# Retention plus GELU feed-forward on one core: a new order of loads with a hold, block 0 in runs of 128 tokens, and the last block's products M6, M1, M7 by halves

## The chip, the cores and the metric

One Trainium2 chip, one of its cores. The metric is device time in microseconds (us) of one execution. The kernel before takes 296.12 us, the median of 3 runs (295.0 to 297.18).

## The reference

Inputs are q, k, v, each 8 batches x 8 heads x 576 positions x 64, and two weight matrices, `w_in` 512 x 2048 and `w_out` 2048 x 512, all float32.

```python
scores = scale * np.matmul(q, k.transpose(0, 1, 3, 2))
gamma = 1.0 - 2.0 ** (-5.0 - np.arange(H))
Dmat = np.where(rel >= 0, gamma[:, None, None] ** rel[None], 0.0)
attn = np.matmul(scores * Dmat[None], v)
x = attn.transpose(0, 2, 1, 3).reshape(B * S, H * D)
h = x @ w_in
out = (0.5 * h * (1.0 + erf(h / sqrt(2)))) @ w_out
```

So: a causal attention without softmax, whose mask decays with distance (retention), then a feed-forward layer with exact GELU over 4608 tokens of 512 values. The output is 4608 x 512, float32.

## The kernel before

**Units, groups, blocks.** A unit is 128 tokens. There are 36: batches go in pairs, and a pair has four chunks of 128 positions for each of its two batches, and one unit for the last 64 positions of both (units 10, 17, 26 and 35). Units 0 to 3 stand alone in groups 0 to 3; from unit 4 on the two units of one chunk form a group, so group 4 is units 4 and 5, group 5 is 6 and 7, group 6 is 8 and 9, group 7 is unit 10, group 8 is 11 and 12, group 9 is 13 and 14. A block is four units, 512 tokens, and there are nine.

**Attention of one group.** `load` brings q, k and v by DMA, issued on POOL and cast to bfloat16 on the way. q and k must be transposed: for groups 0 to 6 by TensorE (`turn`, with a copy out by VectorE or ScalarE), from group 7 on by two DMA transposes per group issued on SP (`turn_dma`). `scores` multiplies them on TensorE, `masked` applies the mask on VectorE (`ret`), `inner` multiplies with the values, `state` gathers the running state of keys and values, `cross` adds the contribution of the earlier chunks, `evacuate` writes the unit's transposed attention output into `xT`.

**Feed-forward.** `mlp1` multiplies `w_in` with `xT` (four matmuls for each 128 columns of `w_in`) and applies GELU on ScalarE. Block 0 takes it in runs of tokens 0 to 256, 256 to 384 and 384 to 512, block 1 in halves, later blocks whole. Block 0 then uses `mlp2`: plain matmuls with `w_out` that add up in one bank of PSUM for each unit (`ts`), in steps of two or four slices `m` of `w_out`; w_out number n holds slices 2n and 2n+1. Blocks 1 to 8 use seven products of half size (a Strassen scheme: M1 to M7, `part` with its four quarters, `after` for what follows each product), in the order M3, M4, M5, M2, M1, M6, M7. The sums of weights are made on VectorE by `sum_w`, those of GELU outputs by `sum_g`. M7 adds onto the bank of M1 (`behind`). In the last block M1 and M7 have a bank for each half; M7 goes half by half, M1 ends both halves together. `store` issues the output DMAs on SP.

**What sets the order.** The kernel is a planner in Python: it keeps a clock for each engine (`T`), costs for operations, a model of two DMA queues (`MOVE`, `SW_LATE`, `HW_LATE`, `SW_SHARE`), and writes out each engine's instructions in the order in which it thinks they can run. On the chip each engine runs its instructions in that fixed order and waits at semaphores where its plan was wrong. The loads up to unit 12, the weights, the constants (`io`) and the decay factors (`dq`) go in an order written out by hand, `ORDER` (lines 306 and 307), which `next_order` (309) takes from; later loads are appended by `reload` (525) as buffers come free. `fire` (786) issues loads, scaled values and DMA transposes; `mlp_pick` (764) chooses the next step of the feed-forward among the heads of the first four `runs`. A step of `mlp2` counts as ready (`mlp_ready`, 754) by this line, 761, in which `b_` and `c_` are the first and the end slice of the step:

```python
at = max(land_out.get((c_ - 1) // 2, 1e9) + SEM, max(g_at.get((t, m, ts), 1e9) for m in range(b_, c_)))
```

POOL issues at most eight loads ahead of the oldest that has not landed; SP issues transposes and stores in one queue. The steps by which the prediction goes: loads at lines 270 (`w_in`), 284 (`w_out`) and 297 (q, k, v); `turn` 387; transposes 398; `scores` 415, 424 and 434; `inner` 482 and 491; `state` 509; `cross` 541; `mlp1` 579; `mlp2` 614; `part` 712; the last sums 679; stores 604.

Of the kernel before, what the change touches and what calls it, by code (L numbers as in the profile page):

```python
# [10 lines left out]
BF16 = mybir.dt.bfloat16  # L11
# [6 lines left out]
def kernel(  # L18
# [14 lines left out]
    nc = tc.nc  # L33
# [35 lines left out]
    N_PE_TR = 7  # L69
# [109 lines left out]

    SW_LATE, HW_LATE, SW_SHARE = 4.6, 2.5, 0.48  # L180
    MOVE = {"wi": 1.28, "wo": 1.37, "ld": 0.845, "short": 0.42, "turn": 1.82, "store": 0.85}
    queues = ([], [])
# [81 lines left out]
    def load(what, i):  # L264
# [26 lines left out]
        for jj in (j,) if j is not None else range(2):  # L291
# [8 lines left out]
            else:  # L300
# [4 lines left out]
    cast_due = {("q", 0): (loaded[0][0][:, 0], first["q32"]), ("k", 0): (loaded[0][0][:, 1], first["k32"])}  # L305
    ORDER = ("k1 q1 wi0 io v0 k2 v2 q2 v1 k3 wi1 q3 wi2 wi3 wi4 k4 v3 q5 k5 wo0 wi5 wi7 wi6 q4 q6 wo1 v4 v5 wo2 "
             "wo3 k7 q7 q8 k6 wo4 dq2 q9 wo5 v6 k9 k11 v9 wo6 dq3 wo7 k8 v7 k10 v10 v12 q11 k12 q12 v8 v11 q10 dq4").split()

    def next_order():
        item = ORDER.pop(0)  # L310
        what = item.rstrip("0123456789")
        load(what, int(item[len(what):] or 0))

    def finish_later():
        while later:
            _, engine, dur, fn = later.pop(0)
            fn()
            on(engine, dur)

    while T["pool"] < 4.0:  # L320
        next_order()
# [71 lines left out]
    def turn_dma(n):  # L393
        qk, qkT = loaded[groups[n][0]][0], qkT_of(n)
        short = units[groups[n][0]][2] is None
        rows = TAIL if short else C
        for jj in range(2):
            nc.sync.dma_start(qkT[:, jj, :, 0:rows], qk[0:rows, jj].rearrange("p h j d -> p (h j d)"), transpose=True)
            ends = sg[n].setdefault("ends", {})

            def put(end, jj=jj):
                ends[jj] = end
                sg[n]["T"] = max(ends.values()) + SEM

            hw_dma(1.3, MOVE["turn"] * (0.5 if short else 1.0), max(land["qk"[jj], i] for i in groups[n]), put)

# [256 lines left out]
    def after(t, p, done, ts0, ts1, b, m):  # L663
# [13 lines left out]
        else:  # L677
            c = c11 if p == M7 else c22
            nc.vector.tensor_tensor(c, c, m, op=MINUS if p == M6 else ALU.add)  # L679
            at = on("dve", 0.26 * (ts1 - ts0) + 0.16, done)  # L680
        read_at[t, p] = at + SEM
        if p not in behind.values():
            release(b, at + SEM)
        if p == M6:
            for x in range(2):
                store(t, 2 + x, hi[:, x, :])
# [10 lines left out]
    def part(t, p, k):  # L697
        apart = t == N_BLK - 1 and p in (M1, M7)
        keys = [(t, bank_of[p], x) for x in range(1 + apart)]
        if p == M3 and k == 0:  # L700
            for x in range(2):
                o_tiles[t, x] = o_pool.tile([128, 2, d_model], FP32, tag=f"o{x}", name=f"o{x}")
        if k == 0 and p in begins:
            for key in keys:
                held_bank[key] = bank([128, 2 - apart, 256], FP32, "m")
        todo = [(mm, ts) for mm in range(2 * k, 2 * k + 2) for ts in range(2)]
        if apart and p == M7:
            todo = [(mm, k // 2) for mm in range(k % 2 * 4, k % 2 * 4 + 4)]
        for mm, ts in todo:
            a, w = factors(t, p, mm, ts)  # L710
            m = held_bank[keys[ts * apart]][1]
            nc.tensor.matmul(m[:, 0 if apart else ts, :], lhsT=a, rhs=w,  # L712
                             start=p in begins and mm == 0 and (apart or ts == 0),
                             stop=p not in behind.values() and mm == N_DF // 2 - 1, skip_group_check=True)
        done = pe(4 * 0.1092)
        if apart and (p == M1 and k == 3 or p == M7 and k % 2):
            for ts in range(2) if p == M1 else (k // 2,):
                after(t, p, done, ts, ts + 1, *held_bank[keys[ts]])
        elif k == 3:
            after(t, p, done, 0, 2, *held_bank[keys[0]])  # L720

    def part_ready(t, p, k):
        mms = range(2 * k, 2 * k + 2)
        at = max(ws_at.get(mm, 1e9) for mm in mms)
        if p in (M3, M4):
            at = max([at] + [g_at.get((t, 2 * mm + x, ts), 1e9) for mm in mms for x in range(2) for ts in range(4)])
        else:
            n = {M2: 0, M5: 0, M1: 1}.get(p, 2)
            if p == M7 and t == N_BLK - 1:
                mms = range(N_DF // 2)  # L730
            at = max([at] + [gs_at.get((t, mm, n), 1e9) for mm in mms])
        if k == 0:
            at = max(at, read_at.get((t, behind[p]), 1e9) if p in behind
                     else free_time(1 + (p == M1 and t == N_BLK - 1)))
        return at
# [5 lines left out]
    for t in range(N_BLK):  # L741
        if t < 2:
            cuts = (0, 256, 384, 512) if t == 0 else (0, 256, 512)
            for lo, hi in zip(cuts, cuts[1:]):
# [6 lines left out]
        else:  # L751
            runs.append([("3", t, p, k) for p in range(7) for k in range(4)])

# [26 lines left out]
    nA = nB = nX = nT = nV = 0  # L780
    nD = N_PE_TR
    half = 0
# [3 lines left out]
    def fire():  # L786
        nonlocal nD, nV
        now = T["pe"]
        while ORDER and T["pool"] <= now + 1.5:
            next_order()  # L790
        while T["dve"] <= now + 1.5:
# [40 lines left out]
    while True:  # L832
# [6 lines left out]

        pick = mlp_pick(1 if runs and runs[0] and runs[0][0][1] > 1 else 4)  # L840
        head = pick[1][0] if pick else None
# [128 lines left out]
```

## Time and profile before

| what | value |
|---|---|
| median of 3 runs | 296.12 us (295.0 to 297.18) |
| the profiled execution | 295.88 us, its span 294.1 us |
| TensorE clock granted in it | 0.998 |
| matmuls busy | 282.1 us of the span |
| VectorE, ScalarE, POOL busy | 193.2, 131.5, 113.8 us |
| q0, DMAs issued on POOL | 18.10 MB |
| q1, DMAs issued on SP | 16.52 MB |

In the profile PE is the row of matmuls, PEld that of weight loads (they overlap), DVE is VectorE, ACT is ScalarE, POOL is GpSimd, SP the engine that issues transposes and stores (SPq: its queue). An arrow `out<-in` names tiles. "Time to landing" is from the start of an issue to the DMA's last part. All times are from the start of the span. Times of 0.25 us or less between matmuls of one step include places where a record is missing.

### The profile page before, as it was taken

How to read it: one execution, taken by the hardware profiler on the slowest of the kernel's cores; microseconds unless marked ns; L12 is line 12 of the kernel's file. 1: busy time of each engine (PE TensorE's matmuls, PEld its weight loads, DVE VectorE, ACT ScalarE, POOL GpSimd, SP SyncE). 2: the span in 40 equal slices, each digit the busy share in tenths (PEclk: the TensorE clock that was granted, in tenths of full speed). 3: DMA queues.
4: the chain of work that ended last, by engine and by line, in shares of the span. 5: the costliest groups of instructions: out<-in, count | busy, mean ns of one | idle time of the engine just before them, and what ended most of it. 6: DMA issues, size and time to landing. Idle time of an engine off the chain costs nothing.

```text
span 294.1 us, 7654 instructions
## 1 busy us (share of the span) xinstructions
PE 282.1 (96%) x3191; PEld 195.2 (66%) x3212; DVE 193.2 (66%) x455; ACT 131.5 (45%) x235; POOL 113.8 (39%) x143
## 2 busy tenths in 40 slices
PE   7999999997899999999999999999999999999993
PEld 2588766586785488558845785578557854874682
DVE  3762387987698983974497789754977385435532
ACT  5476444363215641574065414741554156416620
POOL 8977898975583246510784444000000000000000
PEclk9999999999999999999999999999999999999999
DMA  9999999999999999999999999990300040021013
GB/s 135 162 178 188 181 171 172 200 177 132 137 134 222 141 126 147 190 156 153 79 228 122 121 141 163 196 71 22 125 2 0 4 144 0 0 74 72 0 38 107
DMA packets 152066, 35.36 MB, mean 120 GB/s; under 512 B 141024, under 2 KB 147680, under 8 KB 152032
## 3 DMA queue, kind: packets, MB, share of 16 engines
q0 software_dynamic: 116832, 18.10, 96.0%
q1 hardware_dynamic: 34160, 16.52, 32.7%
q8 instruction: 25, 0.41, 0.6%
q10 hardware_dynamic: 1040, 0.26, 0.4%
q14 instruction: 9, 0.07, 0.1%
HBM read 36.70 MB, written 9.44 MB: 157 GB/s over the span
## 4 chain that ended last, share of the span: by engine, by line
PE 83%; DMA 10%; POOL 4%; issue 1%; DVE 0%; SPq 0%; POOLq 0%; DVEq 0%
PE hT L579 38%; PE m L712 31%; PE oT L614 4%; DMA qkT<-qk_ld 4%; DMA qk_ld<-in_q_dram 3%; DMA w_in<-in_moe_w_in_dram 3%; PE sc L434 3%; PE o_ps L491 3%; POOL qk L297 2%; POOL w_in L270 1%; PE o_ps L541 1%; PE u_ps L509 1%; POOL v_ld L297 1%; PE qk_ps L387 1%; PE sc L424 0%
## 5 line engine op out<-in xcount | busy, mean ns | idle before, releaser
L579 PE MATMUL hT<-xT,w_in 128*128 128x512 bf16 (+2 forms) x754 | 128.0, 325 | 1.0 <-issue 0.2
L586 ACT ACTIVATE g<-hT 128x512 bf16<-128x512 f32 (+1 forms) x152 | 86.8, 574 | 68.5 <-PE hT L579 63.0
L579 PEld LDWEIGHTS <-w_in 128*128 128x128 bf16 x768 | 68.8, 98 | 54.5 <-DMA w_in<-in_moe_w_in_dram 0.3
L712 PEld LDWEIGHTS <-gs 128*128 128x128 bf16 x640 | 62.5, 98 | 7.4
L297 POOL DMA_DIRECT2D v_ld<-in_v_dram x40 | 34.0, 856 | 25.9 <-DVE vh L467 7.0
L712 PE MATMUL m<-w_sum,gs 128*128 128x256 bf16 x384 | 43.4, 273 | 0.0
L457 DVE TENSOR_TENSOR ret<-sc,msk 128x512 bf16<-128x512 f32 x48 | 30.4, 683 | 14.1 <-PE sc L434 14.1
L297 POOL DMA_DIRECT2D qk_ld<-in_q_dram x36 | 30.4, 849 | 23.2 <-DMA qkT<-qk_ld 16.9
L297 POOL DMA_DIRECT2D qk_ld<-in_k_dram x36 | 30.5, 852 | 16.8 <-DMA qk_ld<-in_q_dram 14.8
L639 DVE TENSOR_TENSOR gs<-g 128x512 bf16<-128x512 bf16 x64 | 26.1, 421 | 13.5 <-ACT g L586 13.5
L712 PE MATMUL m<-w_out,gs 128*128 128x256 bf16 x256 | 29.6, 273 | 0.0
L712 PE MATMUL m<-w_sum,g 128*128 128x256 bf16 x256 | 29.6, 273 | 0.0
L712 PEld LDWEIGHTS <-g 128*128 128x128 bf16 x256 | 24.9, 98 | 4.5
L679 DVE TENSOR_TENSOR o<-o,m 128x512 f32<-128x512 f32 (+1 forms) x26 | 16.7, 646 | 16.7 <-PE m L712 16.4
L643 DVE TENSOR_TENSOR gs<-g 128x512 bf16<-128x512 bf16 x64 | 25.5, 418 | 0.0
L467 DVE TENSOR_TENSOR vh<-v_ld,dv 128x512 bf16<-128x512 bf16 x36 | 23.6, 683 | 1.3 <-DMA v_ld<-in_v_dram 1.3
L675 DVE TENSOR_TENSOR o<-o,m 128x512 f32<-128x512 f32 x16 | 11.0, 686 | 14.7 <-ACT o L674 14.7
L370 ACT CAST u_sb<-u_ps 128x512 bf16<-128x512 f32 x14 | 8.2, 585 | 25.3 <-PE u_ps L509 25.3
L560 DVE TENSOR_TENSOR xT<-o_ps,dqT 128x512 bf16<-128x512 f32 (+1 forms) x32 | 18.4, 616 | 1.4 <-PE o_ps L541 1.3
L674 ACT COPY o<-m 128x512 f32<-128x512 f32 x16 | 9.4, 585 | 21.1 <-PE m L712 21.1
L668 ACT COPY o<-m 128x512 f32<-128x512 f32 x16 | 9.4, 585 | 20.9 <-PE m L712 19.5
L641 DVE TENSOR_TENSOR gs<-g 128x256 bf16<-128x256 bf16 x64 | 17.2, 284 | 0.0
(72 smaller groups left out, 193.9 us busy)
## 6 DMA issues: line engine op xcount, KB each, us to landing
out_dram<-o SPq DMA_DIRECT2D x30, 256.0 KB, 4.9
v_ld<-in_v_dram POOLq DMA_DIRECT2D x32, 128.0 KB, 9.5
qk_ld<-in_k_dram POOLq DMA_DIRECT2D x28, 128.0 KB, 10.6
qk_ld<-in_q_dram POOLq DMA_DIRECT2D x28, 128.0 KB, 8.7
w_in<-in_moe_w_in_dram POOLq DMA_DIRECT2D x8, 256.0 KB, 7.6
w_out<-in_moe_w_out_dram POOLq DMA_DIRECT2D x8, 256.0 KB, 7.9
out_dram<-o SPq DMA_DIRECT2D x12, 128.0 KB, 2.4
qk_ld<-in_k_dram POOLq DMA_DIRECT2D x8, 64.0 KB, 11.9
```

What stands on the lines that cost most here:

```text
L297: nc.gpsimd.dma_start(dst, src[2 * bp + jj, :, ci * C:ci * C + n, :].rearrange("h s d -> s h d"))
L457: nc.vector.tensor_tensor(r, t, by, op=ALU.mult)
L467: nc.vector.tensor_tensor(vh, loaded[i][1], dv[:, :, ci:ci + 1].to_broadcast([128, H, D]), op=ALU.mult)
L560: nc.vector.tensor_tensor(x_of(i)[:, :, n * x:n * x + n], o, dqT[:, :, ci * C:ci * C + n], op=ALU.mult)
L579: nc.tensor.matmul(hT[:, m, :], lhsT=w[:, cc, o:o + 128], rhs=x_tiles[t][:, cc, lo:hi], start=(cc == 0), stop=(cc == N_DM - 1))
L586: nc.scalar.activation(g_tiles[t, m0 // 2][:, m0 % 2:m0 % 2 + n, lo:hi], hT, AF.Gelu)
L614: nc.tensor.matmul(oT, lhsT=g_tiles[t, m // 2][:, m % 2, cols], rhs=w_out_sb[m // 2][:, m % 2, :], start=(m == 0), stop=(m == N_DF - 1))
L639: nc.vector.tensor_tensor(s[:, 0:2].rearrange("p a b -> p (a b)"), g[:, 0, :], g[:, 1, :], op=ALU.add)
L641: nc.vector.tensor_tensor(s[:, 2], g[:, 0, LEFT], g[:, 1, RIGHT], op=ALU.add)
L643: nc.vector.tensor_tensor(s[:, 3:5], g[:, :, LEFT], g[:, :, RIGHT], op=MINUS)
L679: nc.vector.tensor_tensor(c, c, m, op=MINUS if p == M6 else ALU.add)
L712: nc.tensor.matmul(m[:, 0 if apart else ts, :], lhsT=a, rhs=w, start=p in begins and mm == 0 and (apart or ts == 0), stop=p not in behind. ...
```

## The change

- `ORDER` is another order of the same loads, with one new item, `h7`, ahead of the last load, v11. At `h7`, `next_order` stops until the transposes of group 7 (unit 10) have been given out, then puts a small copy from their result (tile `rest`) on POOL, which holds all later loads there until these transposes have landed.
- Block 0's `mlp1` goes in four runs of 128 tokens, and `mlp_pick` looks at five runs.
- In the last block the products go in the order M3, M4, M5, M2, M6, M1, M7; M1, too, goes half by half, and the stores of the lower output half follow M1's halves and not M6.
- The planner's numbers for the DMA queues change.

In the order that comes out for TensorE, `mlp2` for unit 2 of block 0 goes slices 8 to 12 and then (after the scores of group 5) 12 to 16 ahead of slices 8 to 16 of units 0 and 1; before, it followed them. The scores of group 7 stand ahead of the last three pieces of block 1's `mlp1` and of its first two quarters of M3; before, behind them. Loads around them, in the new order: ... w_out 3, k9, v6, w_out 5, w_out 7, k10, w_out 4, v9, w_out 6, k8, v7, ...

```diff
@@ -177,8 +177,8 @@
         nc.vector.tensor_tensor(s[:, 3:5], w[:, :, 0:256], w[:, :, 256:512], op=ALU.add)
         ws_at[i] = on("dve", 1.0, land_out[i]) + SEM
-    SW_LATE, HW_LATE, SW_SHARE = 4.6, 2.5, 0.48
-    MOVE = {"wi": 1.28, "wo": 1.37, "ld": 0.845, "short": 0.42, "turn": 1.82, "store": 0.85}
+    SW_LATE, HW_LATE, SW_SHARE = 4.65, 2.8, 0.455
+    MOVE = {"wi": 1.28, "wo": 1.37, "ld": 0.845, "short": 0.42, "turn": 1.88, "store": 0.9}
     queues = ([], [])
     moved = [0.0, [0, 0], [None, None]]
@@ -303,13 +303,23 @@
     tiles_of(0)
     land["q", 0], land["k", 0] = 4.5, 4.6
     cast_due = {("q", 0): (loaded[0][0][:, 0], first["q32"]), ("k", 0): (loaded[0][0][:, 1], first["k32"])}
-    ORDER = ("k1 q1 wi0 io v0 k2 v2 q2 v1 k3 wi1 q3 wi2 wi3 wi4 k4 v3 q5 k5 wo0 wi5 wi7 wi6 q4 q6 wo1 v4 v5 wo2 "
-             "wo3 k7 q7 q8 k6 wo4 dq2 q9 wo5 v6 k9 k11 v9 wo6 dq3 wo7 k8 v7 k10 v10 v12 q11 k12 q12 v8 v11 q10 dq4").split()
+    ORDER = ("q1 k2 io v0 wi0 v3 q3 k1 q2 wi1 k4 k3 v1 wi2 wi3 q5 v2 k5 wi4 wo0 q8 wi5 wo1 q4 wi7 wi6 v4 q6 q7 dq2 "
+             "k7 k11 wo2 v5 k6 q9 wo3 k9 v6 wo5 wo7 k10 wo4 v9 dq3 wo6 k8 v7 v10 q12 k12 dq4 v12 v8 q11 q10 h7 v11").split()
+
+    rest = const.tile([128, 2], BF16, name="rest")
     def next_order():
-        item = ORDER.pop(0)
-        what = item.rstrip("0123456789")
-        load(what, int(item[len(what):] or 0))
+        what = ORDER[0].rstrip("0123456789")
+        n = int(ORDER[0][len(what):] or 0)
+        if what == "h":
+            if n >= nD:
+                return False
+            nc.gpsimd.tensor_copy(rest, qkT_of(n)[:, :, 0, 0])
+            T["pool"] = max(T["pool"], sg[n]["T"]) + 0.2
+        else:
+            load(what, n)
+        ORDER.pop(0)
+        return True
     def finish_later():
         while later:
@@ -317,6 +327,7 @@
             fn()
             on(engine, dur)
+    nD = N_PE_TR
     while T["pool"] < 4.0:
         next_order()
     next_load = [group_of[12] + 1]
@@ -402,7 +413,7 @@
                 ends[jj] = end
                 sg[n]["T"] = max(ends.values()) + SEM
-            hw_dma(1.3, MOVE["turn"] * (0.5 if short else 1.0), max(land["qk"[jj], i] for i in groups[n]), put)
+            hw_dma(1.3, MOVE["turn"] * (0.62 if short else 1.0), max(land["qk"[jj], i] for i in groups[n]), put)
     def scores(n):
         g = groups[n]
@@ -678,11 +689,11 @@
             c = c11 if p == M7 else c22
             nc.vector.tensor_tensor(c, c, m, op=MINUS if p == M6 else ALU.add)
             at = on("dve", 0.26 * (ts1 - ts0) + 0.16, done)
-        read_at[t, p] = at + SEM
+        read_at[t, p, ts0] = at + SEM
         if p not in behind.values():
             release(b, at + SEM)
-        if p == M6:
-            for x in range(2):
+        if p == M1 if t == N_BLK - 1 else p == M6:
+            for x in range(ts0, ts1):
                 store(t, 2 + x, hi[:, x, :])
         if p == M5 and t == N_BLK - 1:
             for x in range(2):
@@ -704,7 +715,7 @@
             for key in keys:
                 held_bank[key] = bank([128, 2 - apart, 256], FP32, "m")
         todo = [(mm, ts) for mm in range(2 * k, 2 * k + 2) for ts in range(2)]
-        if apart and p == M7:
+        if apart:
             todo = [(mm, k // 2) for mm in range(k % 2 * 4, k % 2 * 4 + 4)]
         for mm, ts in todo:
             a, w = factors(t, p, mm, ts)
@@ -713,9 +724,8 @@
                              start=p in begins and mm == 0 and (apart or ts == 0),
                              stop=p not in behind.values() and mm == N_DF // 2 - 1, skip_group_check=True)
         done = pe(4 * 0.1092)
-        if apart and (p == M1 and k == 3 or p == M7 and k % 2):
-            for ts in range(2) if p == M1 else (k // 2,):
-                after(t, p, done, ts, ts + 1, *held_bank[keys[ts]])
+        if apart and k % 2:
+            after(t, p, done, k // 2, k // 2 + 1, *held_bank[keys[k // 2]])
         elif k == 3:
             after(t, p, done, 0, 2, *held_bank[keys[0]])
@@ -726,12 +736,13 @@
             at = max([at] + [g_at.get((t, 2 * mm + x, ts), 1e9) for mm in mms for x in range(2) for ts in range(4)])
         else:
             n = {M2: 0, M5: 0, M1: 1}.get(p, 2)
-            if p == M7 and t == N_BLK - 1:
+            if p in (M1, M7) and t == N_BLK - 1:
                 mms = range(N_DF // 2)
             at = max([at] + [gs_at.get((t, mm, n), 1e9) for mm in mms])
-        if k == 0:
-            at = max(at, read_at.get((t, behind[p]), 1e9) if p in behind
-                     else free_time(1 + (p == M1 and t == N_BLK - 1)))
+        if p in behind and (k == 0 or k == 2 and p == M7 and t == N_BLK - 1):
+            at = max(at, read_at.get((t, behind[p], k // 2), 1e9))
+        elif k == 0:
+            at = max(at, free_time(1 + (p == M1 and t == N_BLK - 1)))
         return at
     def x_ready(t, lo, hi):
@@ -740,7 +751,7 @@
     runs = []
     for t in range(N_BLK):
         if t < 2:
-            cuts = (0, 256, 384, 512) if t == 0 else (0, 256, 512)
+            cuts = (0, 128, 256, 384, 512) if t == 0 else (0, 256, 512)
             for lo, hi in zip(cuts, cuts[1:]):
                 runs.append([("1", t, m, 2, lo, hi) for m in range(0, N_DF, 2)])
         else:
@@ -749,7 +760,8 @@
             runs.append([("2", t, ts, m, m + 2) for m in range(0, N_DF, 2) for ts in range(2)])
             runs.append([("2", t, ts, m, m + 4) for ts in range(2, 4) for m in range(0, N_DF, 4)])
         else:
-            runs.append([("3", t, p, k) for p in range(7) for k in range(4)])
+            turns = (M3, M4, M5, M2, M6, M1, M7) if t == N_BLK - 1 else range(7)
+            runs.append([("3", t, p, k) for p in turns for k in range(4)])
     def mlp_ready(one):
         if one[0] == "1":
@@ -778,7 +790,6 @@
     nA = nB = nX = nT = nV = 0
-    nD = N_PE_TR
     half = 0
     u_due = []
     s_done = set()
@@ -786,8 +797,8 @@
     def fire():
         nonlocal nD, nV
         now = T["pe"]
-        while ORDER and T["pool"] <= now + 1.5:
-            next_order()
+        while ORDER and T["pool"] <= now + 1.5 and next_order():
+            pass
         while T["dve"] <= now + 1.5:
             one = min((x for x in queued if x[0] <= now + 0.2), key=lambda x: x[1], default=None)
             if one is None:
@@ -837,7 +848,7 @@
         def cand(ready, fn, *a):
             acts.append((ready, fn, a))
-        pick = mlp_pick(1 if runs and runs[0] and runs[0][0][1] > 1 else 4)
+        pick = mlp_pick(1 if runs and runs[0] and runs[0][0][1] > 1 else 5)
         head = pick[1][0] if pick else None
         early = nA < 4
         stuck = bool(pick) and pick[0] > now + 0.5
```

## Prediction, made before the changed kernel was run

> **What bounds the kernel now.** I read the page's busy shares and slices first, then the chain of work that ended last, then the timeline of PE around the two thin slices, the timeline of POOL with the DMA view for the loads, and the timeline of the end.
>
> ```profile
> PE 282.1 (96%) x3191; PEld 195.2 (66%) x3212; DVE 193.2 (66%) x455; ACT 131.5 (45%) x235; POOL 113.8 (39%) x143
> PE   7999999997899999999999999999999999999993
> DMA  9999999999999999999999999990300040021013
> PE 83%; DMA 10%; POOL 4%; issue 1%; DVE 0%; SPq 0%; POOLq 0%; DVEq 0%
> ```
>
> PE is full from the second slice to the last but one, so time can be gained or lost only where PE waits: in the first 15 us, near 75 us, and after the last matmul. The loads fill the DMA engines for two thirds of the span, so a load that comes later in the queue lands later by what was put ahead of it. The timeline of PE has the two waits:
>
> ```profile
> 69.23 0.42 PE L509 MATMUL u_ps<-vh,qk 128*64 128x64 bf16 x16
> 69.48 0.42 PE L509 MATMUL u_ps<-vh,qk_ld 128*64 128x64 bf16 x16
> 71.98 0.38 PE L424 MATMUL sc<-qkT 64*64 64x64 bf16 x12 [2.08 <-DMA qkT<-qk_ld]
> ...
> 77.92 0.32 PE L482 MATMUL o_ps<-ret,vh 64*64 64x64 bf16 x16
> 79.39 0.64 PE L434 MATMUL sc<-qkT 64*64 64x128 bf16 x32 [1.16 <-DMA qkT<-qk_ld]
> ```
>
> Sixteen of these small matmuls take 0.25 us (69.23 to 69.48), so PE stood from 69.73 to 71.98 for the scores of group 7, and from 78.17 to 79.39 for those of group 8: 2.25 + 1.22 = 3.47 us. Both times a DMA transpose was late. The DMA view gives these transposes a median of 10.2 us to landing while loads run, and 4.3 us for the two of unit 26, issued between 134 and 140 us as the loads ran out:
>
> ```profile
> qkT<-qk_ld SPq DMA_TRANSPOSE x30, 10.2
> ```
>
> ```profile
> qkT<-qk_ld SPq DMA_TRANSPOSE x2, 4.3
> ```
>
> **1. The hold and the two waits: 3.47 us go.** In the new order the two halves of q10 are the last loads ahead of the hold. In before they landed at 62.81 (55.62 + 7.2); one load (v11, 0.87) and two of three stores (2.8 us for the three: v10 to q10 landed 8.6 us apart, where 5.8 is usual) no longer pass ahead of them, so I estimate 60, at most 62. Unit 10's transposes also stand behind block 0's last store on SP (59.0 in before, about 59.5 now, by step 2). With the loads stopped two such transposes took 4.3 us: they land between 64 and 66.6, those of units 11 and 12 some 4 us later. By step 2 PE wants the first at 71.3 and the second at about 81 (6.2 us from 71.98 to 78.17 in before, and 3.5 us of work that now lies between). So neither waits.
>
> Behind the copy on POOL are v11, q13, q14, k13, k14 and all later loads. Released at 64.3 to 66.6, issued at 0.87 us each, with 3.4 to 5 us to landing (3.4 for the first load after POOL's long wait that ends at 141.73), k14 lands at 72.5 to 75; in before it was 66.63. The transposes for units 13 and 14 then start at 75 at the latest and, at 10.2 us and 2.4 between the two (72.29 and 74.69 in before), land by 87.6; their scores began at 87.72 in before and are wanted at 89.3 now. I count zero; with the longest time to landing in the view, 13.4, it would be 1.5 us.
>
> **2. The new load order: 5.10 us lost.** This is the large term. POOL's timeline has the last two `w_out` loads, the 41st and 42nd in its queue:
>
> ```profile
> 41.03 0.73 POOL L284 DMA_DIRECT2D w_out<-in_moe_w_out_dram  x1
> 41.74 1.08 POOL L278 TENSOR_TENSOR dqT<-dqT,step 128x512 f32<-128x512 f32 x1
> 42.72 0.76 POOL L284 DMA_DIRECT2D w_out<-in_moe_w_out_dram  x1
> ```
>
> and the DMA view, for the one issued at 42.72 alone:
>
> ```profile
> w_out<-in_moe_w_out_dram POOLq DMA_DIRECT2D x1, 256.0 KB, 6.9
> ```
>
> So the 42nd load landed at 49.6. Landings of neighbours in the queue are 1.3 us apart for a `w_out`, 0.87 for a full q, k or v, 0.43 for a half of unit 10, since POOL never has more than eight on their way and the engines are full. In the new order the 42nd load is w_out 4. Ahead of it are the same loads but for one `w_out` and one full load fewer and the two halves of k10 more: 49.6 - 1.3 - 0.87 + 0.85 = 48.3. The 44th is w_out 6: 48.3 + 0.87 (v9) + 1.3 = 50.45.
>
> The new PE order puts slices 8 to 12 of unit 2, which need w_out 4 and 5, ahead of everything else that w_out 4 feeds. The planner asked only for the landing of the last slice's weights (line 761: w_out 5, which now comes three places ahead of w_out 4), so it took the step for ready about 3.5 us too early, and PE, which runs in order, must stand there until 48.3. Then: four matmuls of 512 columns (0.87), the scores of group 5 (0.57), and slices 12 to 16, which the plan let go for w_out 7 but which wait for w_out 6 until 50.5, and take 0.87. At 51.37 PE begins the first step of unit 3.
>
> In before it began this step at 52.80 (the nine matmuls from 51.72 are the last two of unit 1, four of unit 2 and three of unit 3). But by then it had done more: three 256-token pieces of block 1's `mlp1` (3 x 0.874), eight pairs of `mlp2` (8 x 0.433) and two transposes of unit 8 and 9's keys (0.45), 6.53 us in all, which the new order has behind this point. So PE is 6.53 - 1.43 = 5.10 us behind. While it stands, VectorE's and ScalarE's work for group 5 stands too, without price of its own, since it follows PE.
>
> From there to the scores of group 7 PE worked from 52.80 to 69.73 without a wait: 16.93 us. Now the 3.46 and 0.45 us are added and two quarters of M3 (0.87) taken away: 51.37 + 19.97 = 71.3. The units needed are there (v7, 46th in the queue, at 52.2).
>
> Bounds of this term: PE does not reach the step later than 48.3 (part 3), so only the landing counts. If the queue ran as in its slowest stretch (q7 came 0.8 us late) it is 5.9, if 0.8 faster 4.3. I take 5.1.
>
> **3. Block 0 in runs of 128 and the first loads: nothing, up to 2.8 us.** By 22.3 us PE had done twelve 128-token pieces of `mlp1`; now w_in 2, 3 and 4 and v1 and v2 stand later in the queue (v2 at 21.6 in place of 12.1), and units 0 and 1 with w_in 0 to 3 allow eight. That is four pieces of 0.446 us, less the attention of unit 3 already done (0.34). PE then waits about 0.5 us for unit 2's copy to `xT`, and loses no more where it waited before, three times between 29 and 42 us, 1.2 us in all. Without any change it would reach slices 8 to 12 of unit 2 at 45.9 - 1.7 = 44.2 (the scores of group 5 begin at 45.91, with four pairs of 0.433 ahead that are now later); with some 1.3 us lost, at 45.5. The cover is the wait for w_out 4, 2.8 us. ScalarE has 16 more GELU instructions net, 32 x 382 ns against 16 x 382 and 8 x 597: 1.3 us on an engine that is busy for about half of this stretch.
>
> A short run must pay for a weight load of its own. The row:
>
> ```profile
> 23.27 3.30 PE L579 MATMUL hT<-xT,w_in 128*128 128x128 bf16 x56
> ```
>
> 56 of them start within 3.14 us (the next step starts at 26.41), 56 ns each, half of the 109 ns of a 256-token one: 128 in place of 64 add 0.1 us. The Trainium skill ("TensorE: Matmul & The Clock Gate", section "Back-to-back issue gap") says that a stream of weight loads and matmuls of 128 columns sustains one in about 81 ns. By that the change would add 128 x 81 - 64 x 109 = 3.4 us in place of 0.1, of which 2.8 lie under the wait, and the sum would be 0.6 higher, 297.4. The row is of this kernel and shape, so I give that no chance of its own.
>
> **4. The end: 0.7 us gained.** The timeline of the last 12 us:
>
> ```profile
> 282.82 8.00 SPq L604 DMA_DIRECT2D out_dram<-o  x7
> 287.45 0.69 DVE L679 TENSOR_TENSOR o<-o,m 128x512 f32<-128x512 f32 x1 [1.10 <-PE m L712]
> 288.33 0.42 DVE L679 TENSOR_TENSOR o<-o,m 128x256 f32<-128x256 f32 x1 [0.19 <-PE m L712]
> 289.20 0.42 DVE L679 TENSOR_TENSOR o<-o,m 128x256 f32<-128x256 f32 x1 [0.45 <-PE m L712]
> ```
>
> The last sum is ready at 289.62, but SP ends its last issue at 290.82: the three stores of the lower half start at 288.20, after M6, and the last two queue behind them. Now M6 comes before M1, and M1's halves end 2.6 and 1.75 us before PE's last matmul (289.18), at 286.56 and 287.43; their sums (0.42) are done at 287.0 and 287.9, and the three issues (0.4 to 0.6 each) are over by 289.0. The last store goes at 289.7 and no longer at 290.43: 0.7 us. M7's first half needs M1's first bank read by 287.43; it is read at 287.0. The second: 287.9 against 288.3. Cover is thus 0.4 us; if it fails, up to 0.4 of the gain goes. Nothing can be gained beyond 0.8.
>
> **Sum.** 295.88 (the profiled execution, 0.24 under the median) + 5.10 - 3.47 - 0.7 = 296.8, about the median of 296.12.
>
> **The rivals.** (a) *The weights are there in time.* If the loads land as early as the plan says, PE doesn't stand at w_out 4 and 6: 2.8 + 0.7 us less, 293.3. Against it: the queue was always eight deep and its landings evenly spaced, and nothing in the change speeds it. 9%. (b) *The hold starves the attention behind it.* If the transposes of units 13 and 14 move one for one with their loads (k14 5.9 to 8.4 us later, so 90.5 to 93 in place of 84.57), PE waits 1.2 to 3.7 us for the scores at 89.3: 298.0 to 300.5, slower. It decides from a landing at 89.3 on. Against it: in before these transposes queued behind those of group 8, which landed at 79.35 and now are gone by 71. 14%. (c) *The hold does not shorten the transposes*, since three stores stand ahead of them and 10.2 us remain: 59.5 + 10.2 + 1.4 = 71.1, still in time for 71.3. The time is that of the forecast, and group 8, some 4 us behind, is wanted 10 us later. Only the reason would be another: PE's lateness. It lies within the forecast.
>
> **How the numbers follow.** Forecast (c included) 77%, (a) 9%, (b) 14%. The forecast's own range is 295.3 to 298.2: the bounds of step 2 (-0.8, +0.8), 0.4 for the end, 0.4 for the runs' scatter. The range given reaches into (a) and (b): 294.0 to 299.3. A measurement of this kernel tells about 1%, 3 us, from no change: faster means under 293.2, slower over 299.1. Of (a) half counts as faster, of (b) two thirds as slower; 3% and 4% more, out of the forecast's 77, are for what I have not seen on either side.
>
> **What would show it.** Right: on PE a wait for the DMA of `w_out` of 2 to 4 us before 48.3, a second, short one at 50; no wait for `qkT` at 71 and 81; block 1's first step of M3 on PE at about 74.5 (67.69 in before); a gap in POOL of several us before 66; the last store issued within 0.2 us of the last sum. Wrong: PE arrives at w_out 4 after it landed, or waits for `qkT` at 89 or later, at 102 above all.

## The result and the profile after

The changed kernel takes 298.29 us (median of 14 runs, 297.02 to 299.49), the kernel before 296.61 us (14 runs, 295.0 to 298.13) on the same chip: ratio 1.0061, 95% interval 1.0037 to 1.0085. The profiled execution took 298.71 us, span 296.9, against 295.88 and 294.1: the two profiles lie 2.83 us apart, the medians 1.68, so what follows accounts for this pair of executions and overstates the usual difference.

The page of the changed kernel, rows of busy time, slices and chain:

```profile
PE 285.3 (96%) x3280; PEld 196.3 (66%) x3280; DVE 193.7 (65%) x453; ACT 134.1 (45%) x245; POOL 114.3 (39%) x144
PE   7999995999999999999999999999999999999994
DMA  9999999979999999999999999900300040003013
PE 81%; DMA 10%; POOL 6%; issue 1%; DVE 0%; ACT 0%; POOLq 0%
```

The thin place of PE has moved: the tenth and eleventh slices (66 to 81 us), which stood at 7 and 8, are full now, and the seventh (44.5 to 52 us) is at 5. The chain still runs over PE. The timeline of PE at the two old places and the new ones (start, length, engine, line, operation, tiles, count, idle time before with what ended it):

```profile
49.46 1.02 PE L625 MATMUL oT<-w_out,g 128*128 128x512 bf16 x4 [2.47 <-DMA w_out<-in_moe_w_out_dram]
50.41 0.64 PE L445 MATMUL sc<-qkT 64*64 64x128 bf16 x32
51.59 1.67 PE L625 MATMUL oT<-w_out,g 128*128 128x512 bf16 x7 [0.54 <-DMA w_out<-in_moe_w_out_dram]
...
72.29 0.38 PE L435 MATMUL sc<-qkT 64*64 64x64 bf16 x12
...
82.32 0.58 PE L445 MATMUL sc<-qkT 64*64 64x128 bf16 x27 [0.17 <-DVE o L686]
...
89.22 0.25 PE L552 MATMUL o_ps<-qkT,u_sb 64*64 64x128 bf16 x3 [0.57 <-issue]
```

The scores of group 7 (72.29) have no idle time ahead, those of group 8 (81.88, second part 82.32) no DMA wait. In their place PE stands for `w_out` twice, ahead of 49.46 and of 51.59, and two short waits are new: for a bank of PSUM that VectorE empties late (82.32), and within group 8's `cross` (89.22), where the profile shows nothing that PE waits for (`issue`).

I compare the two kernels at equal work: the start of a step, less the full-rate time of all steps that PE has done before it. From group 8 on both have done the same work, and the difference is that of the starts. After less before:

| where | PE behind by | what has come |
|---|---|---|
| `mlp2` unit 3, first step | 5.97 us | w_out 4 and 6, block 0's start |
| scores of group 7 | 3.81 | the old first qkT wait is gone |
| scores of group 8, 81.88 | 2.49 | the second is gone |
| the step of M2 behind them, 82.96 | 2.87 | the wait at 82.32 |
| past 89.4, to the last matmul | 3.60 | the wait at 89.22 |
| last store | 2.90 | the end, 0.70 shorter |

POOL's timeline, the loads of w_out 4 and 6 and the hold:

```profile
42.05 0.74 POOL L284 DMA_DIRECT2D w_out<-in_moe_w_out_dram  x1
...
45.17 0.75 POOL L284 DMA_DIRECT2D w_out<-in_moe_w_out_dram  x1
...
66.34 0.53 POOL L317 COPY rest<-qkT 128x2 bf16<-128x2 bf16 x1 [10.94 <-DMA qkT<-qk_ld]
```

The line of w_out 4, issued at 42.05, in the DMA view of 42.0 to 42.5 (columns: tiles, queue, operation, count, size, us to landing):

```profile
w_out<-in_moe_w_out_dram POOLq DMA_DIRECT2D x1, 256.0 KB, 7.4
```

It lands at 49.42, and the wait ends at 49.46. POOL then stands still from 55.4 to 66.34. The transposes issued in that pause (units 10 to 12, issues at 61.06 to 66.17) and the next two (units 13 and 14, 73.40 and 74.99), by the DMA view of windows of their own:

```profile
qkT<-qk_ld SPq DMA_TRANSPOSE x4, 3.5
```

```profile
qkT<-qk_ld SPq DMA_TRANSPOSE x2, 8.3
```

In before the four of units 10 to 12 had a median of 8.1 us. So a transpose in the pause takes less than half as long, and afterwards it is slow again. The end:

```profile
286.42 7.31 SPq L615 DMA_DIRECT2D out_dram<-o  x7
...
292.80 0.42 DVE L690 TENSOR_TENSOR o<-o,m 128x256 f32<-128x256 f32 x1 [0.45 <-PE m L723]
```

The last sum ends at 293.22 and the last issue on SP at 293.73; in before these were 289.62 and 290.82. The last sum is 3.60 us later, the last issue 2.91: that is the 0.70 of the table.

### The profile page after: what moved, and what is told of

Same layout as the page of the kernel before. It is cut to its first block, busy times and chain, and to the rows that moved or that the text cites. A ratio compares the mean times of both kernels' runs of the same rounds, so it can differ in the third digit from the quotient of the medians.

```text
span 296.9 us, 7819 instructions
## 1 busy us (share of the span) xinstructions
PE 285.3 (96%) x3280; PEld 196.3 (66%) x3280; DVE 193.7 (65%) x453; ACT 134.1 (45%) x245; POOL 114.3 (39%) x144
## 4 chain that ended last, share of the span: by engine, by line
PE 81%; DMA 10%; POOL 6%; issue 1%; DVE 0%; ACT 0%; POOLq 0%
PE hT L590 37%; PE m L723 33%; DMA w_in<-in_moe_w_in_dram 6%; DMA w_out<-in_moe_w_out_dram 5%; PE oT L625 3%; PE o_ps L502 2%; PE sc L445 2%; POOL qk L297 2%; POOL v_ld L297 1%; PE u_ps L520 1%; POOL qk_ld L297 1%; PE o_ps L552 1%; POOL w_in L270 1%; PE sc L435 0%; POOL dqT L278 0%
## 5 line engine op out<-in xcount | busy, mean ns | idle before, releaser
L590 PE MATMUL hT<-xT,w_in 128*128 128x512 bf16 (+2 forms) x832 | 129.4, 314 | 0.6 <-ACT xT L381 0.5
L597 ACT ACTIVATE g<-hT 128x512 bf16<-128x512 f32 (+1 forms) x160 | 88.5, 555 | 69.2 <-PE hT L590 63.1
L590 PEld LDWEIGHTS <-w_in 128*128 128x128 bf16 x832 | 69.9, 98 | 54.3 <-DMA w_in<-in_moe_w_in_dram 0.4
L381 ACT CAST u_sb<-u_ps 128x512 bf16<-128x512 f32 x15 | 8.8, 585 | 25.8 <-PE u_ps L520 25.8
L625 PE MATMUL oT<-w_out,g 128*128 128x512 bf16 x64 | 14.9, 379 | 3.0 <-DMA w_out<-in_moe_w_out_dram 3.0
```

The source lines that it names most:

```text
L590: nc.tensor.matmul(hT[:, m, :], lhsT=w[:, cc, o:o + 128], rhs=x_tiles[t][:, cc, lo:hi], start=(cc == 0), stop=(cc == N_DM - 1))
L597: nc.scalar.activation(g_tiles[t, m0 // 2][:, m0 % 2:m0 % 2 + n, lo:hi], hT, AF.Gelu)
L625: nc.tensor.matmul(oT, lhsT=g_tiles[t, m // 2][:, m % 2, cols], rhs=w_out_sb[m // 2][:, m % 2, :], start=(m == 0), stop=(m == N_DF - 1))
```

## The experiments

All are ratios to the kernel before on the same chip, with 95% intervals. A ratio is not the quotient of the two medians; the two differ by up to 0.004 here. My theory going in: the loss sits at w_out 4 and 6, because the planner asks for the landing of the last slice's weights only, and the hold is worth nothing because PE is late anyway. The rival: the hold does the work of removing the waits. "Theory" and "rival", or A and B, are those of each experiment's own expectation.

**The weights waited for in the plan.** The changed kernel with one line of the planner altered:

```diff
-            at = max(land_out.get((c_ - 1) // 2, 1e9) + SEM, max(g_at.get((t, m, ts), 1e9) for m in range(b_, c_)))
+            at = max(max(land_out.get(m // 2, 1e9) for m in range(b_, c_)) + SEM, max(g_at.get((t, m, ts), 1e9) for m in range(b_, c_)))
```

> The changed kernel, but the planner asks for the landing of the weights of every slice of an mlp2 step, and not of the last slice alone. It then gives out pieces of block 1's mlp1 ahead of slices 8 to 12 of unit 2. My theory (the new load order costs its time in the waits for w_out 4 and 6, 2.63 and 0.70 us in the profile after): both waits go, nothing takes their place since the transposes of units 10 to 12 land 5 us ahead of need, and the time falls by about 3.2 us, ratio to the kernel before 0.995. Rival (the loads bound this stretch, so work moved ahead only shifts the wait): PE waits 2 to 3 us a few steps later, at w_out 4, at v7 or at the transposes, and the time stays within 0.5 us of the changed kernel, ratio 1.004 to 1.006.

Measured: 296.37 us, 0.9954 (0.9921 to 0.9988). The view of PE's waits:

```profile
PE o_ps L552 <- issue: 1.4, 1, 1.4
...
PE hT L590 <- DMA w_in<-in_moe_w_in_dram: 1.1, 1, 1.1
```

No wait for `w_out` is left, though w_out 4 and 6 land as late as in the changed kernel (49.43 and 51.60); the planner fills the place with four more pieces of block 1's `mlp1`. So the wait at w_out 4 and 6 is what makes the changed kernel slower, and it is the plan that puts it there, not the queue.

**The hold taken out of the order.** `h7` deleted from `ORDER`, all else as changed:

```diff
-             "k7 k11 wo2 v5 k6 q9 wo3 k9 v6 wo5 wo7 k10 wo4 v9 dq3 wo6 k8 v7 v10 q12 k12 dq4 v12 v8 q11 q10 h7 v11").split()
+             "k7 k11 wo2 v5 k6 q9 wo3 k9 v6 wo5 wo7 k10 wo4 v9 dq3 wo6 k8 v7 v10 q12 k12 dq4 v12 v8 q11 q10 v11").split()
```

> The changed kernel without the hold: the item h7 is taken out of the load order, v11 stays last. My theory (PE is late at the scores of group 7 and 8 by itself, so the transposes need no hold): their transposes take 10 us in place of 4 and land at about 71 and 77, PE wants them at 72.3 and 81.8, and the time is that of the changed kernel within 0.7 us, ratio to before 1.004 to 1.008. Rival (the hold is what removed the two waits): they come back, up to 2.25 and 1.2 us, ratio 1.013 to 1.018.

Measured: 301.77 us, 1.015 (1.0103 to 1.0197). I had expected no change of the time: a miss. The lost time lies behind group 8. Without `h7` the planner takes the later loads to land earlier, and PE now has group 9's scores (87.72) ahead of group 8's `inner` (90.82), and group 10's at 96.4 in place of 104.0; VectorE's timeline there:

```profile
88.22 1.48 DVE L690 TENSOR_TENSOR o<-o,m 128x512 f32<-128x512 f32 x2
89.61 2.48 DVE L468 TENSOR_TENSOR ret<-sc,msk 128x512 bf16<-128x512 f32 x4
92.01 1.28 DVE L478 TENSOR_TENSOR vh<-v_ld,dv 128x512 bf16<-128x512 bf16 x2
93.21 0.68 DVE L690 TENSOR_TENSOR o<-o,m 128x512 f32<-128x512 f32 x1
```

These follow each other without a pause, and PE waits for `vh` behind the mask of the next group. From 86 to 94 us VectorE is busy for 7.68 of 8, PE for 5.93, ScalarE for nothing: no `mlp1` lies in between. In before VectorE is as full there (7.78), but PE (7.95) has `mlp1` to do meanwhile (ScalarE 3.45). This is a loss of another plan and does not tell what the hold itself is worth, so the next run keeps the plan.

**The same plan without the copy.** Only the copy on POOL is deleted; every engine's order stays:

```diff
-            nc.gpsimd.tensor_copy(rest, qkT_of(n)[:, :, 0, 0])
```

> The changed kernel with its plan kept, and the copy that holds POOL left out: each engine has the same instructions in the same order, only the copy from unit 10's transposes is missing on POOL, so the loads behind it aren't held. It tells why the kernel without the item h7 was 1.5% slower than before. Theory A (its plan was worse, not the missing hold: without h7 the planner puts the scores of groups 9 and 10 some 7 us earlier, and PE lost 3.8 us around them): here the transposes of unit 10 land at about 72.5, at the moment PE wants them, those of units 11 and 12 at 79, before 81.8, and the ratio to before is 1.004 to 1.009, that of the changed kernel. Rival (the missing hold itself): the loads that now run beside the transposes make PE wait 2 us and more at the scores of groups 7 to 10, ratio 1.013 or more.

Measured: 298.26 us, 1.0069 (1.0038 to 1.0101), as with the copy (1.0061). The transposes of units 10 to 12 land at 72.5 and 78.9 in place of 66.2 and 69.3, and PE still loses only this much:

```profile
PE sc L434 <- DMA qkT<-qk_ld: 0.7, 1, 0.7
```

Theory held: in the changed kernel the hold has no measurable worth; the intervals would hide about 0.4%. The trace alone would not show it. In this execution w_out 4 landed 1.7 us earlier (47.74), and TensorE's clock then stood at half for 3.4 us from 49.0 on (last section), so PE came to group 7 about as late as in the changed kernel, but in another way.

**The same with the weights in time.** Is it worth something where PE is not late? The planner's line of the first experiment, again without the copy and with its plan kept:

> The variant whose plan waits for the landing of every w_out slice, with the same plan and the same order on every engine, only the hold's copy on POOL deleted. Theory A (the hold is worth nothing in the changed kernel only because PE is late there): this variant wants the scores of group 7 at 70.8 and of group 8 at 78.7, as in its profile; without the copy the transposes land as they did where the copy alone was deleted (72.5 and 78.9), so PE waits 1 to 2.5 us for qkT again, and 0.5 to 2 us of it are left at the end: ratio 0.999 to 1.002, against 0.9954 with the copy. Rival B (the hold is worth nothing anywhere; what is won at groups 7 and 8 is given back at group 9): 0.994 to 0.997.

Measured: 298.44 us, 1.0055 (1.0027 to 1.0083) against 0.9954 with the copy; rival B is out, and the effect is larger than theory A had it. The timeline of PE shows the wait back:

```profile
72.03 0.38 PE L435 MATMUL sc<-qkT 64*64 64x64 bf16 x12 [1.75 <-DMA qkT<-qk_ld]
```

The two profiled executions differ by 1.0 us only (spans 295.6 and 294.6), the medians by 2.07. Against the 1.75 us stand two differences that no edit made: this execution was 0.64 us ahead at 61 us (`mlp1` from 61.19, in the other from 61.83), and PE's unexplained stop in group 8's `cross` took 1.05 us in place of 1.45.

**The new order alone.** The kernel before with the new `ORDER`, without `h7`:

> The kernel before with the new order of loads and nothing else, no hold (the planner then writes its own PE order). Theory A (the new order costs about 5 us at the w_out slices, and of the two qkT waits nothing is left because PE comes late): before + 5 to 6 - 3.5 and 1 for new short waits, 298.5 to 300, ratio 1.006 to 1.012, a PE wait for w_out of 2 to 4 us near 48. Rival B (without the hold's item the planner issues later loads early and the plan goes astray in the scores of groups 9 and 10, as it did with the changed kernel without the hold): 1.015 to 1.02.

Measured: 301.41 us, 1.0178 (1.0131 to 1.0225): rival B. Both losses are in its trace: PE idle for 2.39 us ahead of 48.12, for `w_out`, as in theory A, and the attention of two groups without `mlp1` between (from 86 to 94 us VectorE 7.28, PE 5.62, ScalarE 0.59).

**The old order with the hold.** The kernel before with `next_order` and `fire` as changed, and:

```diff
-             "wo3 k7 q7 q8 k6 wo4 dq2 q9 wo5 v6 k9 k11 v9 wo6 dq3 wo7 k8 v7 k10 v10 v12 q11 k12 q12 v8 v11 q10 dq4").split()
+             "wo3 k7 q7 q8 k6 wo4 dq2 q9 wo5 v6 k9 k11 v9 wo6 dq3 wo7 k8 v7 k10 v10 v12 q11 k12 q12 v8 v11 q10 dq4 h7").split()
```

> The kernel before with the hold alone, at the end of its old load order (after q10 and the last decay factor). Here PE reaches the scores of group 7 at 69.7, 2.6 us earlier than in the changed kernel. With my theory (loads stopped, the transposes of unit 10 land about 5 us after q10, at 68, those of units 11 and 12 at 72): both waits go, 3.4 us, and nothing starves behind it: ratio 0.989. Rival (the loads held back come too late for units 13 to 16): PE waits 1 to 4 us for the scores of groups 9 and 10, and the ratio is 0.993 to 1.003.

Measured: 0.9877 (0.9819 to 0.9935), as theory had it. Here the transposes of units 10 to 12 land by 67.1 and 70.3, and PE, 6 us earlier than in the changed kernel (the step of M2 behind group 8's scores at 76.87, there 82.96), waits for neither. It waits behind the hold instead, which theory had excluded:

```profile
87.19 1.07 PE L445 MATMUL sc<-qkT 64*64 64x128 bf16 x32 [2.70 <-DMA qkT<-qk_ld]
```

That is the mechanism of rival (b), in a kernel whose PE is early enough. This execution is the slowest of its six (296.7 us, mean clock 0.994; the others 292.5 to 294.1, clock 0.998 to 1.0); whether those wait there as long can't be seen.

**The end alone, and both.** The kernel before with the last block's part of the diff (`turns`, the stores behind M1, M1 and M7 by halves):

> The kernel before with the last block's part of the change alone: order M3, M4, M5, M2, M6, M1, M7, M1 and the stores of the lower half by halves. My theory (the last store no longer queues behind those of the lower half): 0.7 us faster, ratio 0.9977; the last store is issued within 0.2 us of the last sum. Rival (the stores' transfers bound the end, not their issue): the end after the last matmul stays 4.9 us, ratio 1.000.

Measured: 0.9983 (0.9945 to 1.002). 0.7 us would be 0.9976; it agrees but is not told from nothing. The trace shows the step that was forecast: SP's last issue starts 0.13 us behind the last sum's end (291.05 and 290.92), in before 0.81 (290.43 and 289.62). With the hold in the old order as well:

> The kernel before with the hold at the end of its old load order and the last block by halves: the two parts that gained, without the new order and the runs of 128. My theory: 3.6 us from the hold alone and 0.7 from the end add up, ratio 0.984 to 0.987. Rival (the gain of the hold is given back at the scores of group 9, where the profile of the hold alone showed a wait of 2.7 us): 0.990 to 0.997.

Measured: 293.89 us, 0.9922 (0.9888 to 0.9955), in the rival's range: faster than both kernels, not told from the hold alone. Its wait at group 9:

```profile
87.27 0.64 PE L445 MATMUL sc<-qkT 64*64 64x128 bf16 x32 [2.38 <-DMA qkT<-qk_ld]
```

**Runs of 128 tokens alone.** The kernel before with:

```diff
-            cuts = (0, 256, 384, 512) if t == 0 else (0, 256, 512)
+            cuts = (0, 128, 256, 384, 512) if t == 0 else (0, 256, 512)
-        pick = mlp_pick(1 if runs and runs[0] and runs[0][0][1] > 1 else 4)
+        pick = mlp_pick(1 if runs and runs[0] and runs[0][0][1] > 1 else 5)
```

> The kernel before with block 0's four runs of 128 tokens (and the look over five runs) alone. My theory (a 128-token matmul costs half of a 256-token one, GELU has room): within 0.7 us, ratio 0.997 to 1.003, with the waits for the transposes at 70 and 78 us as before. Rival (short runs pay for their weight loads, 81 ns for each of them): 3.4 us slower, ratio 1.011; or they let PE begin earlier, 1 to 2 us faster until the next late load.

Measured: 1.0016 (0.9979 to 1.0053). The short runs cost nothing that can be measured. Of the two waits for the transposes its trace has the first (1.97 us at 71.75) and not the second: the clock stood at half behind the first, and PE came late to group 8.

**The changed kernel with the old order.** All of the change but the order, with `h7` at the end:

> The changed kernel with the old load order in place of the new one, the hold kept at its end. My theory (the new order is the whole loss, the other parts gain or are even): as fast as the hold and the end alone, ratio 0.984 to 0.988. Rival (the runs of 128 or the planner's new numbers cost too): 0.992 or more.

Measured: 306.2 us, 1.0331 (1.0293 to 1.0369), far from what I expected. Up to block 4's first M3 it is no slower than the hold and end on the old order (161.30 us, there 162.84); at block 6's it is 11.5 us behind (233.77 against 222.31). PE's longest wait:

```profile
PE o_ps L502 <- DVE vh L478: 4.4, 1, 4.4
```

It stands 4.4 us ahead of 212.53 for `vh`, and of the 11.5 us some 3.4 go to a halved clock (6.83 us at half, last section). The planner's new costs (`MOVE`, `SW_LATE`, `HW_LATE`, `SW_SHARE`) are the part not tried alone; that they lead the plan there is a guess.

**Two attempts at group 9.** q10 ahead of v8 and v11, on the old order with hold and new end, so that the hold opens earlier:

```diff
-             "wo3 k7 q7 q8 k6 wo4 dq2 q9 wo5 v6 k9 k11 v9 wo6 dq3 wo7 k8 v7 k10 v10 v12 q11 k12 q12 v8 v11 q10 dq4 h7").split()
+             "wo3 k7 q7 q8 k6 wo4 dq2 q9 wo5 v6 k9 k11 v9 wo6 dq3 wo7 k8 v7 k10 v10 v12 q11 k12 q12 q10 v8 v11 dq4 h7").split()
```

> The old order with the hold and the new end, but unit 10's q ahead of v8 and v11, so that the hold opens earlier. Theory A (the 2.5 us wait at the scores of group 9 follows the hold's end, one for one): the hold opens 1.7 to 2 us earlier, the transposes of units 13 and 14 land at 85 in place of 87.2, the wait shrinks to under 1 us: ratio 0.986 to 0.989, against 0.9922 where q10 comes last. Rival B (after the hold the loads come in a burst and these transposes take their 10 us whenever they start, and the planner, seeing an earlier landing, moves their scores up as well): the wait stays over 1.5 us, ratio 0.991 to 0.996.

Measured: 1.0012 (0.998 to 1.0044). The transposes of units 13 and 14 did land 4.1 us earlier (83.10), but the planner moved their scores up too, and PE still waits (1.54 us at 83.14), then for `vh` (0.70 at 86.91) and at group 10 (0.67 at 96.46). Rival B, and worse. And a second hold behind k14, on the same kernel:

```diff
-        ORDER.extend(f"{what}{i}" for what in "qkv" for i in groups[next_load[0]])
+        for what in "qkv":
+            ORDER.extend(f"{what}{i}" for i in groups[next_load[0]])
+            if what == "k" and next_load[0] == 9:
+                ORDER.append("h9")
```

> The old order with the hold and the new end, and a second hold behind k14: loads past it wait until the transposes of units 13 and 14 end. Theory A (those transposes are slow because loads pass beside them): they take 3 to 5 us in place of 8 to 10, land by 80 to 82, and the 2.5 us wait at the scores of group 9 goes; the later loads have slack: ratio 0.984 to 0.988. Rival B (the second hold only moves the shortage on to units 15 and 16): the wait at group 9 goes but one of 1.5 us or more appears at the scores of group 10 or behind, ratio 0.992 to 1.0.

Measured: 298.1 us, 1.0049 (1.0019 to 1.008). These transposes now take 3.4 us (landed at 78.57), and the wait at group 9's scores is gone, both as in theory A. But v13, v14 and all later loads are held, and PE pays there:

```profile
87.33 0.41 PE L502 MATMUL o_ps<-ret,vh 128*64 128x128 bf16 x8 [1.91 <-DVE vh L478]
...
102.13 1.05 PE L445 MATMUL sc<-qkT 64*64 64x128 bf16 x32 [2.15 <-DMA qkT<-qk_ld]
```

So rival B, and again worse than its range: a second pause only moves the shortage one group on.

## Why the prediction was right, and where it was off

The forecast was 296.8 us for 298.29 measured: inside the range given (294.0 to 299.3), with the sign of the difference right and its size too small. It is a little above the forecast's own range (295.3 to 298.2), in the part that was there for rival (b), which did not come; so it is partly luck that the number lies inside. By its steps:

- **Step 1, the two waits go, 3.47 us: the size right, the cause only in part.** They went (2.16 and 1.32 us of the offset), and the times of landing were as forecast: q10 at 59.86, unit 10 at 65.16 and 66.20, units 11 and 12 at 68.04 and 69.31, k14 at 74.94, units 13 and 14 at 84.73. But I booked the gain to the hold. With the same plan and no copy the time is the same: PE comes some 6 us late, and the transposes that end at 72.5 and 78.9 are nearly in time for it. What the prediction kept as (c) was true of the time, though not of the transposes, which the hold did shorten (3.5 us against 8.1).
- **Step 2, the new order, 5.10 us: measured 5.97.** The mechanism was right: the step let go for w_out 5 stood for w_out 4, a second wait for w_out 6 followed, and the planner's line was the reason. The sum has a slip: in before unit 3's first step is the seventh matmul from 51.72, at 53.01 and not 52.80, so by its own terms the loss was 4.89. The rest is the weights: w_out 4 landed at 49.42 and not 48.3, w_out 6 at 51.55 and not 50.45. The queue was already 0.95 us late at w_out 0 (26.14 against 25.19) with the same 18 loads ahead. That belongs to this execution and not to the order: in the six traces with the new order w_out 4 lands between 47.74 and 49.43, and the third load, v0, 0.8 to 2.8 us behind the second (here 2.77). The forecast lies within that, and what differs between these executions is not settled. Block 1's first step of M3 came at 75.52, about 74.5 forecast; for before the trace has it at 67.79, not 67.69.
- **Not in the sum: two short waits, 1.11 us.** The first, 0.38, is for the bank at the scores of group 8. It stands in all twelve traces whose scores of group 8 do not wait for `qkT`, five with the old order and the hold among them, and in neither of the two that do wait (before, the end alone). So the old wait covered it, and its 1.22 us were worth only some 0.84: the prediction looked at what PE waits for from DMA, and not at what stood behind that wait. The second, 0.73 in `cross` of group 8, has no cause that a trace shows. It is no step of the plan, since without the copy the same order on PE passes there without a pause:

```profile
88.54 0.42 PE L551 MATMUL o_ps<-qkT,u_sb 64*64 64x128 bf16 x16
```

  It comes and goes between executions: 1.45 us in the first experiment, and 1.28 in the runs of 128 tokens with the old order.
- **Step 3, runs of 128 tokens and first loads, nothing: right.** PE came to the step at 46.83 (45.5 forecast), 2.6 us ahead of the weights, so the cover held, and alone the runs cost nothing (1.0016). One row of the changed kernel has 120 of these matmuls in 7.07 us:

```profile
23.80 7.07 PE L590 MATMUL hT<-xT,w_in 128*128 128x128 bf16 x120 [0.46 <-ACT xT L381]
```

  That is 59 ns each, end included, against the 81 ns of the Trainium skill ("TensorE: Matmul & The Clock Gate", "Back-to-back issue gap"): the row decides here.
- **Step 4, the end, 0.7 us: right to a tenth** in the profile.
- **The rivals.** (a) did not come: the loads were later than forecast, not earlier. (b) did not come either, since PE was late: scores of group 9 at 91.25, landing at 84.73. On the old order with the hold it came, 1.5 to 2.7 us in four traces.

Sum of the terms as measured, on the profiled execution: 295.88 + 5.97 - 3.48 + 1.11 - 0.70 = 298.78, against 298.71.

## What to carry to other kernels

A step that reads several loads is ready when the last of them has landed; a planner that asks only for the one with the highest number fails as soon as the loads are reordered. Where the same edit removes a wait and makes the waiting engine late, the two gains are one: ask whether the wait would have gone by lateness alone, and test it with the instruction order kept. A wait that goes is worth its length less the wait that it covered (1.22 less 0.38 us here). In a kernel whose order comes out of a planner, an edit that should matter in one place can move the plan elsewhere by more than its own worth (1.015, 1.0331), so look first at where the lost time begins.

## What the runs showed of the hardware

**A wait of 2 us can cost 1.7 us more.** The clock granted to TensorE fell to half behind some of PE's waits. The new order alone, windows around its w_out wait (columns: window, its length, then busy us of PE, PEld, DVE, ACT and POOL; then granted clock, DMA share, GB/s):

```profile
46.00:48.00 2.00, 0.00 (x0) 0.00 (x0) 0.00 (x0) 0.36 (x1) 1.93 (x4) 1.00 1.72 182
48.00:49.00 1.00, 0.88 (x4) 0.29 (x3) 0.00 (x0) 0.00 (x0) 1.00 (x2) 0.86 1.82 183
49.00:50.00 1.00, 1.00 (x26) 0.64 (x28) 0.00 (x0) 0.00 (x0) 1.00 (x2) 0.50 2.24 157
50.00:51.00 1.00, 0.97 (x19) 0.47 (x11) 0.63 (x2) 0.00 (x0) 1.00 (x2) 0.50 2.41 153
51.00:52.00 1.00, 0.81 (x2) 0.30 (x2) 1.00 (x3) 0.00 (x0) 1.00 (x3) 0.50 2.41 153
52.00:53.00 1.00, 1.00 (x6) 0.48 (x5) 1.00 (x3) 0.59 (x1) 1.00 (x2) 0.93 2.43 155
```

PE idles to 48.12; from 48.7 on the clock is 0.50, for (0.14 + 3 x 0.50 + 0.07) / 0.50 = 3.42 us. The scores at 49.36 take 1.07 us there, in the changed kernel, at full clock, 0.64. In the other traces that have such a dip it adds up to the same 3.4 us each time, or twice that in the changed kernel with the old order, behind its 4.4 us wait: about 1.7 us of work lost for each 3.4. The fourteen traces have eleven waits of PE of 1.9 us or more; a dip begins near the end of eight of them (1.91 to 4.41 us), from 0.4 us before it to 1.2 behind it, and of none of the shorter waits. Three have none: 2.08 us in before, 2.38 in the hold with the end, 2.47 in the changed kernel. So it strikes some executions and not others. Of the 79 executions of the kernel before in the experiments, the 50 with a mean clock of at most 0.995 have a median span of 295.5 us, the 29 above it 293.9; one dip of 1.71 in 294 us is 0.006 of the mean clock. Of the first experiment's executions (longest wait on PE 1.45 us) ten of twelve are above 0.995. So a kernel with shorter waits can gain more than a pair of profiles without a dip shows: its profiled span (294.6) is not below that of before (294.1, mean clock 0.998), its ratio is 0.9954.

The Trainium skill ("TensorE: Matmul & The Clock Gate", "HAM oscillation — how this bites in real kernels") asks for no idle gap above about 3.4 us. The length of the dips agrees with that figure; here gaps of 1.9 to 2.7 us were enough in part of the executions, and the measurement decides. What in an execution decides it is not shown here: only profiled executions can be looked into.

**Transposes and loads.** The DMA transposes of units 10 to 12 had a median of 2.9 to 3.7 us to landing with the load queue held (the changed kernel and six variants) and of 8.1 to 10.1 us beside running loads (before, and six variants without the hold or its copy).
